# Multi-head attention with mixed heads: the softmax weights applied two steps after the scores, and q·k as three products of high and low parts

## The chip, the cores and the metric

The kernel runs on one NeuronCore of a Trainium2 chip. The metric is the time of one execution on the device, in microseconds (us); lower is better. Engines are written as the profile writes them: PE is TensorE's matmuls, PEld its weight loads, DVE is VectorE, ACT is ScalarE, POOL is GpSimd, SP is SyncE (which here only issues DMAs). Each engine executes its own instructions in program order.

## The reference, cut to what matters

Three layers follow each other: an attention with heads mixed before and after the softmax, a dense feed-forward layer, and a mixture of 8 experts. The change touches the attention alone.

```python
batch, n_heads, seq, head_dim = 4, 12, 448, 64
scores = scale * np.matmul(q, k.transpose(0, 1, 3, 2))
scores = np.einsum('bhij,hg->bgij', scores, w_pre)
scores = scores - np.max(scores, axis=-1, keepdims=True)
attn = np.exp(scores)
attn = attn / (np.sum(attn, axis=-1, keepdims=True) + 1e-09)
attn = np.einsum('bhij,hg->bgij', attn, w_post)
return np.matmul(attn, v).astype(np.float32)
```

Behind it the 1792 tokens of 768 numbers go through the dense layer (`x @ w_in`, 768 to 2048, an activation, `@ w_out`), and each token through one expert of 8 (768 to 1024 to 768).

## The kernel before

The queries of a batch are cut into tiles of 120 (three) and 88 (one), 16 tiles t in all. For each tile and each pair of heads p (six), `qk` makes two matmuls, one for each head of the pair, on rows 0 to 63 and 64 to 127 of PE's array. Both operands are float32, and each such matmul leaves two records in the trace. `qk_ev` scales the two results on ACT and DVE into `so`, and a DMA writes them to `S` in DRAM. The mixing of heads wants (query, head) on the partitions, so `relay` reads them back as `G`, three steps ahead of use (LEAD).

The rest goes by steps s of 20 queries (two units a of 10), 92 steps, 23 in a batch; four of them have 8 queries and one unit. A step's work:

- `premix`: PE, four matmuls with `wp`, mixed scores in PSUM (`psm`)
- `maxi`: DVE, the row maximum (`st`); `exp`: ACT, the exponential `E` and its sums
- `weights`: DVE, 1/sum (two short instructions), then POOL, `M` = `wq` times that, one for each unit
- `post`: PE, 32 small matmuls of `E` with `M` into `psa` (one buffer of two banks)
- `post_ev`: unit 0 by ACT, unit 1 by DVE, copies of `psa` into `AT`
- `av`, `av_ev`: PE, `AT` times the values of the tile before; a DVE copy `X` and a DMA to `x_dram`

The order is written out by hand in the loop at the end of `attention`. In round s it issues premix, maxi and exp of s, then post and post_ev of s-1, then av and qk of other tiles (lists in `at`: `qk` of tile t runs four steps and more before tile t-1 ends, `av` of a tile in the steps of the next one), then weights of s. `dma_k`, `dma_q` and `dma_v` load keys, queries and values some steps ahead. From round 89 on, `beside()` puts in the first work of the dense layer: the loads and decoding of its weights on DVE (`decode`), their splits into two float32r parts on ACT and POOL, and its first matmuls (L268, float32r, 128x128 by 128x448).

[...]

Of the kernel before, what the change touches and what calls it, by code (L numbers as in the profile page):

```python
# [6 lines left out]
F32 = mybir.dt.float32  # L7
F32R = mybir.dt.float32r
# [3 lines left out]
ALU = mybir.AluOpType  # L12
# [23 lines left out]
LEAD, AHEAD = 3, 4  # L36

def attention(tc, qT, kT, vT, w_pre, w_post, x_out, beside=None):


    nc=tc.nc
    tiles=[(b,i0,min(TI,S-i0)) for b in range(B) for i0 in range(0,S,TI)]
    steps=[]; first={}
# [4 lines left out]
    units=lambda s: range((steps[s][2]+9)//10)  # L48
# [6 lines left out]
    wf=pool(front,name="af",bufs=1,side="right"); pq=pool(front,name="pq",bufs=2,space=PS,side="right")  # L55
# [4 lines left out]
    def load_mix():  # L60
# [3 lines left out]
        for c in range(2):  # L64
# [2 lines left out]
            sel(out=x,in_=x,pattern=[[12,5],[0,12]],compare_op=ALU.is_ge,fill=0.0,base=11,channel_multiplier=-1)  # L67
            sel(out=y,in_=y,pattern=[[0,12],[-12,5]],compare_op=ALU.is_ge,fill=0.0,base=0,channel_multiplier=1)
            sel(out=y,in_=y,pattern=[[0,12],[12,5]],compare_op=ALU.is_ge,fill=0.0,base=11,channel_multiplier=-1)
    K={}; V={}; Q={}; St={}; G={}; PM={}; E={}; ST={}; M2={}; PA={}; AT={}; PV={}; QP={}; ready=set(); moved=set()  # L70
    def dma_k(b,p,n=2):
        t=wf.tile([128,2,S],F32,tag="K",bufs=6,name="K") if p%2==0 else K[b,p-1][1]
        for i in range(n): K[b,p+i]=(t[:,(p+i)%2],t)
        nc.sync.dma_start(out=t[:,p%2:p%2+n],in_=kT[b,2*p:2*p+2*n].rearrange("(p h) d s -> (h d) p s",h=2))
    def dma_v(b,h):
        t=w.tile([128,3,4,D],F32,tag="V",bufs=8,name="V")
        for i in range(3): V[b,h+i]=t[:,i]
        nc.sync.dma_start(out=t,in_=vT[b,:,h:h+3])
    def dma_q(t,z=None):
        b,i0,n=tiles[t]  # L80
        if t not in Q: Q[t]=wf.tile([128,6*TI],F32,tag="Q",bufs=2,name="Q")
        lo,hi=(0,6*n) if z is None else z
        nc.sync.dma_start(out=Q[t][:,lo:hi],in_=qT[b,:,6*i0+lo:6*i0+hi])
    def qk(t,p):
        b,i0,n=tiles[t]
        for z in range(2):
            r=slice(64*z,64*z+64)
            QP[t,p,z]=pq.tile([TI,S],F32,tag="q",name="psq")
            nc.tensor.matmul(QP[t,p,z][:n],Q[t][r,p*n:p*n+n],K[b,p][0][r],start=True,stop=True)  # L89
    def qk_ev(t,p):  # L90
# [29 lines left out]
    def weights(s):  # L120
        u=len(units(s)); st=ST[s]
        nc.vector.tensor_scalar_add(st[:,2,0:u],st[:,1,0:u],1e-9)
        nc.vector.reciprocal(st[:,3,0:u],st[:,2,0:u])  # L123
        for a in units(s):
            M2[s,a]=w.tile([124,60],F32,tag="M2",bufs=4,name="M2")
            nc.gpsimd.tensor_scalar_mul(M2[s,a],wq,st[:,3,a:a+1])  # L126
    def post(s,a):
        e,m=E.pop((s,a)),M2.pop((s,a))
        if a==0: PA[s]=pa.tile([128,2,512],F32,tag="a",name="psa")
        for cc in range(4):  # L130
            for cp in range(2):
# [4 lines left out]
    def post_ev(s,a):
        t,k,_=steps[s]
        if t not in AT: AT[t]=w.tile([128,4,12,TI],F32,tag="AT",bufs=2,name="AT")
        i=k+10*a
        o=AT[t][:,:,:,i:i+10].rearrange("p c g (r q) -> p r (c g) q",r=2)  # L140
        x=PA[s][:,:,240*a:240*a+240].rearrange("p r (m q) -> p r m q",q=5)
        if a==0: nc.scalar.copy(o,x)  # L142
        else: nc.vector.tensor_copy(o,x)  # L143
        ready.add((s,a))
    def av(t,p):
        b,i0,n=tiles[t]; l=first[t+1]-1
        if any((l,a) not in ready for a in units(l)): raise RuntimeError('values before weights')
        if p%3==0: PV[t,p//3]=pv.tile([128,3,TI],F32,tag="v",name="psv")
        ps=PV[t,p//3]
        for j in range(4):  # L150
            for z in range(2): nc.tensor.matmul(ps[64*z:64*z+64,p%3,:n],V[b,2*p+z][:,j,:],AT[t][:,j,2*p+z,:n],start=j==0,stop=j==3)  # L151
    def av_ev(t,p):
        if p%3<2: return
        b,i0,n=tiles[t]; x=w.tile([128,3,TI],F32,tag="X",bufs=3,name="X")
        nc.vector.tensor_copy(x[:,:,:n],PV.pop((t,p//3))[:,:,:n])  # L155
        nc.sync.dma_start(out=x_out[b,:,p-2:p+1,i0:i0+n],in_=x[:,:,:n])
    from collections import defaultdict
    at={k:defaultdict(list) for k in 'qakvd'}
    for t in range(NT):
        b=tiles[t][0]; n=first[t+1]-first[t]  # L160
        if t>1:
            for p in range(6): at['q'][first[t-1]-AHEAD+p*(first[t]-first[t-1])//6].append((t,p))
            at['d'][max(0,first[t-1]-AHEAD-4)].append((t,))
        m=first[t+2]-first[t+1] if t+1<NT else 3
        for p in range(6): at['a'][first[t+1]+1+p*m//6].append((t,p))
        if t%4==0 and b>0:
            for p in (0,2,4): at['k'][first[t-1]-AHEAD-9+p].append((b,p))
        if t%4==0:
            for h in (0,3,6,9): at['v'][first[t]+h//3].append((b,h))

    dma_q(0,(0,2*TI)); dma_k(0,0,1); dma_k(0,1,1); dma_q(0,(2*TI,6*TI)); dma_k(0,2); dma_k(0,4)
    dma_q(1)
    load_mix()
    for t in range(2):
        for p in range(6): qk(t,p); qk_ev(t,p)
        if t==0:
            for s in range(LEAD): relay(s)
    for s in range(0,NS+5):
        on=s<NS
        if s+LEAD<NS: relay(s+LEAD)  # L180
        for x in at['d'][s]: dma_q(*x)
        for x in at['k'][s]: dma_k(*x)
        for x in at['v'][s]: dma_v(*x)
        if on:
            premix(s)
            for a in units(s): maxi(s,a); exp(s,a)
        if 0<=s-1<NS:
# [669 lines left out]
```

## Time and profile before

| | us |
|---|---|
| median of 3 runs | 1334.84 (1334.59 to 1337.12) |
| the profiled execution, its time | 1341.98 |
| its span | 1340.3 |
| PE busy | 1217.9 (91%) |
| PEld busy | 992.6 (74%) |
| DVE busy | 787.0 (59%) |
| ACT busy | 606.5 (45%) |
| POOL busy | 312.7 (23%) |

Busy shares are means over three layers. Attention fills about the first 440 us, the beginning of the dense layer (its weights are decoded on DVE) the next 160 or so, and the dense and expert layers the rest. The profiled execution lies 7.1 us above the median of the runs.

### The profile page before, as it was taken

The numbers are of one execution on the slowest core, as the hardware profiler recorded it, in microseconds if no ns is written. First come the engines' busy times: TensorE is split into PE (matmuls) and PEld (weight loads), VectorE is DVE, ScalarE is ACT, GpSimd is POOL, SyncE is SP. The second block draws the span as 40 slices with busy tenths as digits, with TensorE's granted clock in tenths as the row PEclk, the third lists the DMA queues.
The fourth block names the chain that finished last, engine by engine and source line by source line (L and its number), as shares of the span: only waits on it lengthen the run. The fifth ranks groups of instructions, "written<-read, shape, count | busy, mean of one in ns | idle before, by whom it ended". The sixth has DMA issues, their size and how long they took to land. (4 is left out here: it accounts for less than half of the span.)

```text
span 1340.3 us, 31619 instructions
## 1 busy us (share of the span) xinstructions
PE 1217.9 (91%) x13086; PEld 992.6 (74%) x13087; DVE 787.0 (59%) x1340; ACT 606.5 (45%) x1203; POOL 312.7 (23%) x385
## 2 busy tenths in 40 slices
PE   7798998898888788779999999999996979999996
PEld 2355555555555577668899899989996979999996
DVE  1565665565655799997543544454437645566663
ACT  2455555555554444434434433443334534445552
POOL 0111111111111555553121112112113202321110
PEclk9899999999999798989999999999997989999998
DMA  7887987987966355420100010000555756656500
GB/s 222 254 242 208 296 239 212 269 254 202 281 186 203 128 203 194 152 96 26 42 22 21 1 52 11 21 1 11 183 198 172 207 160 190 190 198 228 187 20 21
DMA packets 97825, 201.09 MB, mean 150 GB/s; under 512 B 29711, under 2 KB 67733, under 8 KB 97292
## 3 DMA queue, kind: packets, MB, share of 16 engines
q1 hardware_dynamic: 91596, 186.84, 45.4%
q0 software_dynamic: 6080, 12.18, 2.9%
q8 instruction: 104, 1.70, 0.5%
q14 instruction: 45, 0.37, 0.1%
HBM read 143.60 MB, written 56.43 MB: 149 GB/s over the span
## 5 line engine op out<-in xcount | busy, mean ns | idle before, releaser
L268 PE MATMUL psh<-x,ws 128*128 128x448 f32 x1152 | 264.1, 382 | 25.2 <-POOL ws L260 14.9
L268 PEld LDWEIGHTS psh<-x,ws 128*128 128x128 f32 x1152 | 224.5, 197 | 56.0 <-POOL ws L260 20.3
L285 PE MATMUL pso<-g,ws 128*128 128x448 f32 x1152 | 252.7, 369 | 0.0
L285 PEld LDWEIGHTS pso<-g,ws 128*128 128x128 f32 x1152 | 213.8, 188 | 20.1
L135 PEld LDWEIGHTS psa<-M,E 60*64 60x64 f32 x5760 | 98.2, 138 | 115.2 <-POOL M L126 103.7
L119 ACT ACTIVATE E<-psm,st 124x448 f32<-124x448 f32 x180 | 112.5, 629 | 127.3 <-DVE st L116 127.2
L126 POOL TENSOR_SCALAR M<-wq,st 124x60 f32<-124x60 f32 x180 | 78.7, 451 | 354.8 <-DVE st L123 270.1
L260 DVE TENSOR_TENSOR ws<-res,ws 128x768 fp32r<-128x768 f32 x81 | 91.4, 1128 | 105.8 <-ACT ws L259 102.8
L135 PE MATMUL psa<-M,E 60*64 60x60 f32 x5760 | 108.9, 224 | 48.7 <-POOL M L126 43.1
L278 POOL TENSOR_TENSOR g<-th,g 128x448 fp32r<-128x448 f32 x64 | 78.4, 1225 | 308.2 <-ACT g L277 308.1
L661 PE MATMUL psh<-xt,ws 128*128 128x256 f32 (+2 forms) x1152 | 147.7, 289 | 0.1
L661 PEld LDWEIGHTS psh<-xt,ws 128*128 128x128 f32 x1152 | 145.3, 190 | 0.3 <-DVE xt L653 0.3
L628 DVE TENSOR_TENSOR ws<-res,ws 128x768 fp32r<-128x768 f32 x128 | 121.9, 959 | 39.7 <-ACT ws L627 39.5
L143 DVE COPY AT<-psa 128x480 f32<-128x480 f32 x88 | 60.2, 685 | 133.1 <-ACT AT L142 133.1
L89 PE MATMUL psq<-K,Q 64*120 64x448 f32 (+1 forms) x384 | 114.8, 648 | 11.9 <-ACT so L94 7.0
L116 DVE TENSOR_REDUCE st<-psm 124x1 f32<-124x448 f32 x180 | 103.7, 617 | 14.6 <-PE psm L112 13.8
L680 PE MATMUL psy<-ws,hh 128*128 128x384 f32 x576 | 110.4, 345 | 0.0
L627 ACT CAST ws<-res 128x768 fp32r<-128x768 f32 x128 | 105.5, 832 | 7.9 <-PE psy L697 4.9
L259 ACT CAST ws<-res 128x768 fp32r<-128x768 f32 x108 | 89.9, 832 | 35.5 <-DVE res L254 35.5
L151 PE MATMUL psv<-AT,V 128*64 128x120 f32 (+1 forms) x1536 | 98.8, 273 | 6.9 <-DVE X L155 3.5
L680 PEld LDWEIGHTS psy<-ws,hh 128*128 128x128 f32 x576 | 100.9, 190 | 0.0
L112 PE MATMUL psm<-G,wp 60*64 60x448 f32 x720 | 94.5, 578 | 0.5 <-ACT E L119 0.5
(178 smaller groups left out, 1289.5 us busy)
## 6 DMA issues: line engine op xcount, KB each, us to landing
res<-in_wm SPq DMA_DIRECT2D x56, 768.0 KB
G<-S SPq DMA_DIRECT2D x176, 210.0 KB
S<-so SPq DMA_DIRECT2D x72, 420.0 KB
wd<-in_w_in SPq DMA_DIRECT2D x10, 768.0 KB
wd<-in_w_out SPq DMA_DIRECT2D x10, 768.0 KB
S<-so SPq DMA_DIRECT2D x24, 308.0 KB
V<-in_vT SPq DMA_DIRECT2D x16, 384.0 KB
K<-in_kT SPq DMA_DIRECT2D x11, 448.0 KB
```

Source lines behind the costliest of these rows:

```text
L89: nc.tensor.matmul(QP[t,p,z][:n],Q[t][r,p*n:p*n+n],K[b,p][0][r],start=True,stop=True)
L112: nc.tensor.matmul(PM[s,a][64*c:64*c+64],wp[r],G[s][r,c,:],start=True,stop=True)
L116: nc.vector.reduce_max(ST[s][:,0,a:a+1],PM[s,a][:124],axis=AX.X,negate=True)
L119: nc.scalar.activation(E[s,a],PM.pop((s,a))[:124],AF.Exp,bias=ST[s][:,0,a:a+1],scale=1.0,accum_out=ST[s][:,1,a:a+1])
L135: nc.tensor.matmul(PA[s][64*cp:64*cp+64,c,240*a+60*cc:240*a+60*cc+60],e[r,j:j+64],m[r],start=True,stop=True)
L151: for z in range(2): nc.tensor.matmul(ps[64*z:64*z+64,p%3,:n],V[b,2*p+z][:,j,:],AT[t][:,j,2*p+z,:n],start=j==0,stop=j==3)
L268: nc.tensor.matmul(ps[:,:TB],t[:,wz,c],x[:,xz,:],start=k==0,stop=k==17); k+=1
L285: nc.tensor.matmul(OB[b][o][:,:TB],t[:,wz,c],g[:,xz,:],start=f==0 and k==0,stop=f==NF-1 and k==2)
L627: nc.scalar.copy(t[:,0,:],r[:,c])
L628: nc.vector.tensor_tensor(out=t[:,1,:],in0=r[:,c],in1=t[:,0,:].bitcast(F32),op=ALU.subtract)
L661: nc.tensor.matmul(ps,w[:,a,k*128:(k+1)*128],x[:,b,:],start=k==0 and (a,b)==(0,0),stop=k==5 and a==1)
L680: nc.tensor.matmul(PY[e][2*c+z],h[:,a,c*CP:c*CP+CP],w[:,b,z*384:z*384+384],start=f==0 and k==0,stop=f==7 and k==2)
```

## The change

- Round s now issues post and post_ev of step s-2, then weights of s-1, then av, qk and the evictions of qk. Before it was post and post_ev of s-1, av, qk, weights of s. The loop has one round more, and `av` comes one step later.
- `post_ev` is cut by c (the two banks of `psa`) instead of by unit: c=0 by ACT, c=1 by DVE, and the copies into one `AT` tile are declared independent of each other.
- For tiles 2 to 15, `qk` is six matmuls instead of two: for both heads high q by high k, then high q by low k, then low q by high k, in float32r. Tiles 0 and 1 keep the two float32 matmuls (`raw`).
- `split` makes the parts: for k of a pair of pairs (128x896) a copy on ACT and a subtraction on POOL, 12 times; for q of a tile (128x720 or 528) a copy on DVE and a subtraction on POOL, 14 times. The raw loads go to `kr` and `qr`, two rounds earlier than before; three of the k splits stand ahead of the loop.

```diff
+    def split(k,d,x,shape,bufs,n=None):
+        r=R.pop(k)
+        h,l=(wf.tile(shape,F32R,tag=x+i,bufs=bufs,name=x+i) for i in 'hl')
...
+        if x=='K': nc.scalar.copy(h,r)
+        else: nc.vector.tensor_copy(h,r)
+        nc.gpsimd.tensor_tensor(out=l,in0=r,in1=h.bitcast(F32),op=ALU.subtract)
...
-    def qk(t,p):
-        b,i0,n=tiles[t]
-        for z in range(2):
-            r=slice(64*z,64*z+64)
-            QP[t,p,z]=pq.tile([TI,S],F32,tag="q",name="psq")
-            nc.tensor.matmul(QP[t,p,z][:n],Q[t][r,p*n:p*n+n],K[b,p][0][r],start=True,stop=True)
+    def qk(t,p,raw=False):
+        b,i0,n=tiles[t]; i=slice(p*n,p*n+n)
+        for z in range(2): QP[t,p,z]=pq.tile([TI,S],F32,tag="q",name="psq")
+        if raw: pairs=((R['q',t],R['k',b,p//2]),)
+        else: (qh,ql),(kh,kl)=Q[t,],K[b,p//2]; pairs=((qh,kh),(qh,kl),(ql,kh))
+        for x,(q,k) in enumerate(pairs):
+            for z in range(2):
+                r=slice(64*z,64*z+64)
+                nc.tensor.matmul(QP[t,p,z][:n],q[r,i],k[r,p%2],start=x==0,stop=x==len(pairs)-1)
...
-        o=AT[t][:,:,:,i:i+10].rearrange("p c g (r q) -> p r (c g) q",r=2)
-        x=PA[s][:,:,240*a:240*a+240].rearrange("p r (m q) -> p r m q",q=5)
-        if a==0: nc.scalar.copy(o,x)
-        else: nc.vector.tensor_copy(o,x)
+        o=AT[t][:,:,:,k:k+10*u].rearrange("p x g (a c q) -> p a c (x g) q",c=2,q=5)[:,:,c]
+        x=PA[s][:,c,0:240*u].rearrange("p (a m q) -> p a m q",a=u,q=5)
+        e=nc.scalar.copy if c==0 else nc.vector.tensor_copy
+        i=e(o[:,0],x[:,0]) if u==1 else e(o,x)
+        for j in WA[t]: tc.declare_no_dep(i.ins,j,reason="distinct queries")
...
-            at['d'][max(0,first[t-1]-AHEAD-4)].append((t,))
+            at['d'][max(0,first[t-1]-AHEAD-6)].append((t,)); at['D'][max(0,first[t-1]-AHEAD-2)].append((t,))
...
-        for p in range(6): at['a'][first[t+1]+1+p*m//6].append((t,p))
+        for p in range(6): at['a'][first[t+1]+2+p*m//6].append((t,p))
...
-    for s in range(0,NS+5):
+    for p in (0,2,4): split_k(0,p)
+    for s in range(0,NS+6):
...
-        if 0<=s-1<NS:
-            for a in units(s-1): post(s-1,a)
-            for a in units(s-1): post_ev(s-1,a)
+        if 0<=s-2<NS:
+            for a in units(s-2): post(s-2,a)
+            for c in range(2): post_ev(s-2,c)
+        if 0<=s-1<NS: weights(s-1)
         for x in at['a'][s]: av(*x); av_ev(*x)
         for x in at['q'][s]: qk(*x)
-        if on: weights(s)
         for x in at['q'][s]: qk_ev(*x)
+        for x in at['K'][s]: split_k(*x)
+        for x in at['D'][s]: split_q(*x)
```

How the rows move is seen best where the loop begins. On PE, at the first rounds, before (psq is the result of qk, psm of premix, psa of post, and M with its number the weights of one unit of a step):

```order
L89 MATMUL psq<-K,Q 120x448 x24
L112 MATMUL psm<-G,wp 64x448 x8
L135 MATMUL psa<-M_236,E 64x60 x16
L135 MATMUL psa<-M_238,E 64x60 x16
L112 MATMUL psm<-G,wp 64x448 x4
L135 MATMUL psa<-M_296,E 64x60 x16
L135 MATMUL psa<-M_298,E 64x60 x16
L89 MATMUL psq<-K,Q 120x448 x2
```

The same place on PE in the changed kernel (Kh, Kl, Qh, Ql are the high and low parts):

```order
L102 MATMUL psq<-kr,qr 120x448 x24
L125 MATMUL psm<-G,wp 64x448 x12
L148 MATMUL psa<-M_270,E 64x60 x16
L148 MATMUL psa<-M_272,E 64x60 x16
L102 MATMUL psq<-Kh,Qh 120x448 x2
L102 MATMUL psq<-Kl,Qh 120x448 x2
L102 MATMUL psq<-Kh,Ql 120x448 x2
L125 MATMUL psm<-G,wp 64x448 x4
L148 MATMUL psa<-M_332,E 64x60 x16
```

Three premixes (12 matmuls) now run before the first post, where there were two, and a call of qk is three rows of two.

On DVE, at the same first rounds, before (st is maximum and sum, AT the copy of post, so the eviction of qk):

```order
L95 TENSOR_SCALAR so<-psq 120x448 x12
L116 TENSOR_REDUCE st<-psm 124x1 x2
L122 TENSOR_SCALAR st<-st 124x2
L123 RECIPROCAL st<-st 124x2
L116 TENSOR_REDUCE st<-psm 124x1 x2
L143 COPY AT<-psa 128x2x48x5
L122 TENSOR_SCALAR st<-st 124x2
```

and in the changed kernel:

```order
L108 TENSOR_SCALAR so<-psq 120x448 x12
L129 TENSOR_REDUCE st<-psm 124x1 x2
L80 CAST Qh<-qr 128x720
L129 TENSOR_REDUCE st<-psm 124x1 x2
L135 TENSOR_SCALAR st<-st 124x2
L136 RECIPROCAL st<-st 124x2
L129 TENSOR_REDUCE st<-psm 124x1 x2
L156 COPY AT<-psa 128x2x48x5
```

The reciprocal of a step now stands behind the maxima of the next step, and a copy of q stands between the maxima of rounds 0 and 1.

On PE, at the end of attention (psh is the dense layer's first matmul, psv is av), before:

```order
L135 MATMUL psa<-M_6913,E 64x60 x16
L151 MATMUL psv<-AT,V 64x120 x8
L135 MATMUL psa<-M_6982,E 64x60 x16
L151 MATMUL psv<-AT,V 64x120 x8
L268 MATMUL psh<-x,ws 128x448 x18
L151 MATMUL psv<-AT,V 64x88 x16
```

and in the changed kernel:

```order
L148 MATMUL psa<-M_7369,E 64x60 x16
L166 MATMUL psv<-AT,V 64x120 x8
L286 MATMUL psh<-x,ws 128x448 x18
L148 MATMUL psa<-M_7427,E 64x60 x16
L166 MATMUL psv<-AT,V 64x120 x8
L286 MATMUL psh<-x,ws 128x448 x18
```

The last post moved behind the dense layer's first 18 matmuls.

## Rows read from the trace of the kernel before

**Rows 1.** Two stretches: us, busy of PE, PEld, DVE, ACT, POOL, clock, DMA share, GB/s

```profile
42.00:428.00 386.00, 339.93 (x7828) 200.74 (x7823) 230.27 (x541) 206.01 (x514) 71.19 (x171) 0.98 0.83 236
460.00:600.00 140.00, 111.59 (x516) 94.20 (x516) 138.75 (x125) 57.58 (x81) 72.33 (x61) 0.91 0.46 165
```

**Rows 2.** Who waited for whom, us in total, times, longest: 42 to 428 us

```profile
DVE AT L143 <- ACT AT L142: 127.0, 84, 3.3
...
PE psa L135 <- POOL M L126: 35.2, 49, 1.5
...
PEld psm L112 <- DMA G<-S: 16.6, 25, 0.7
...
PEld psa L135 <- issue: 11.0, 26, 1.9
```

**Rows 3.** Timeline, 262 to 268 us: start, duration, instruction, idle before and its releaser

```profile
262.49 0.98 PE L112 MATMUL psm<-G,wp 60*64 60x448 f32 x8
...
263.57 1.16 DVE L116 TENSOR_REDUCE st<-psm 124x1 f32<-124x448 f32 x2
...
265.53 0.64 ACT L142 COPY AT<-psa 128x480 f32<-128x480 f32 x1
...
266.20 0.69 DVE L143 COPY AT<-psa 128x480 f32<-128x480 f32 x1 [1.47 <-ACT AT L142]
...
267.32 0.83 POOL L126 TENSOR_SCALAR M<-wq,st 124x60 f32<-124x60 f32 x2 [3.28 <-DVE st L123]
...
267.81 0.33 PEld L135 LDWEIGHTS psa<-M,E 60*64 60x64 f32 x16 [1.12 <-POOL M L126]
```

**Rows 4.** Timeline of PE, 300 to 312 us: one step without a wait

```profile
307.64 0.98 PE L112 MATMUL psm<-G,wp 60*64 60x448 f32 x8
308.44 1.11 PE L135 MATMUL psa<-M,E 60*64 60x60 f32 x64
309.48 1.04 PE L151 MATMUL psv<-AT,V 128*64 128x120 f32 x16
310.45 1.02 PE L89 MATMUL psq<-K,Q 64*120 64x448 f32 x4
311.40 0.98 PE L112 MATMUL psm<-G,wp 60*64 60x448 f32 x8
```

**Rows 5.** Groups of instructions by form, 42 to 428 us: busy us, mean ns, idle before

```profile
L112 PE MATMUL psm<-G,wp 60*64 60x448 f32 x678 | 87.0, 571 | 0.0
...
L89 PE MATMUL psq<-K,Q 64*120 64x448 f32 x240 | 64.4, 604 | 1.9 <-ACT so L94 1.9
...
L112 PE MATMUL psm<-G,wp 36*64 36x448 f32 x6 | 2.9, 562 | 0.0
```

**Rows 6.** The page's costliest groups: dense layer's float32r matmuls and splits

```profile
L285 PE MATMUL pso<-g,ws 128*128 128x448 f32 x1152 | 252.7, 369 | 0.0
L285 PEld LDWEIGHTS pso<-g,ws 128*128 128x128 f32 x1152 | 213.8, 188 | 20.1
...
L259 ACT CAST ws<-res 128x768 fp32r<-128x768 f32 x108 | 89.9, 832 | 35.5 <-DVE res L254 35.5
```

**Rows 7.** Timeline, 0 to 48 us: the first loads and the first rounds

```profile
1.30 0.89 SPq L74 DMA_DIRECT2D K<-in_kT  x2
...
4.04 1.85 PE L89 MATMUL psq<-K,Q 64*120 64x448 f32 x4 [4.04 <-DMA K<-in_kT]
...
39.70 0.42 SPq L83 DMA_DIRECT2D Q<-in_qT  x1
...
40.77 1.14 DVE L116 TENSOR_REDUCE st<-psm 124x1 f32<-124x448 f32 x2
```

**Rows 8.** Timeline, 415 to 475 us: the end of attention

```profile
445.42 1.82 POOL L260 TENSOR_TENSOR ws<-re,ws 128x768 fp32r<-128x768 f32 x1
...
447.20 1.84 POOL L228 TENSOR_TENSOR x<-xs,x 128x448 fp32r<-128x448 f32 x1
...
453.51 4.70 PE L268 MATMUL psh<-x,ws 128*128 128x448 f32 x18
```

More of the change, by code (lines that the diff above doesn't have):

```diff
@@ L69, in load_mix, with split_k, split_q @@
             sel(out=y,in_=y,pattern=[[0,12],[12,5]],compare_op=ALU.is_ge,fill=0.0,base=11,channel_multiplier=-1)
-    K={}; V={}; Q={}; St={}; G={}; PM={}; E={}; ST={}; M2={}; PA={}; AT={}; PV={}; QP={}; ready=set(); moved=set()
+    R={}; K={}; V={}; Q={}; St={}; G={}; PM={}; E={}; ST={}; M2={}; PA={}; AT={}; PV={}; QP={}; WA={}; ready=set(); moved=set()
     def dma_k(b,p,n=2):
-        t=wf.tile([128,2,S],F32,tag="K",bufs=6,name="K") if p%2==0 else K[b,p-1][1]
-        for i in range(n): K[b,p+i]=(t[:,(p+i)%2],t)
-        nc.sync.dma_start(out=t[:,p%2:p%2+n],in_=kT[b,2*p:2*p+2*n].rearrange("(p h) d s -> (h d) p s",h=2))
+        if p%2==0: R['k',b,p//2]=wf.tile([128,2,S],F32,tag="kr",bufs=3,name="kr")
+        nc.sync.dma_start(out=R['k',b,p//2][:,p%2:p%2+n],in_=kT[b,2*p:2*p+2*n].rearrange("(p h) d s -> (h d) p s",h=2))
+    def split(k,d,x,shape,bufs,n=None):
+        r=R.pop(k)
+        h,l=(wf.tile(shape,F32R,tag=x+i,bufs=bufs,name=x+i) for i in 'hl')
+        if n is not None: r,h,l=r[:,:n],h[:,:n],l[:,:n]
+        if x=='K': nc.scalar.copy(h,r)
+        else: nc.vector.tensor_copy(h,r)
+        nc.gpsimd.tensor_tensor(out=l,in0=r,in1=h.bitcast(F32),op=ALU.subtract)
+        d[k[1:]]=(h,l)
+    def split_k(b,p): split(('k',b,p//2),K,'K',[128,2,S],6)
+    def split_q(t): split(('q',t),Q,'Q',[128,6*TI],2,6*tiles[t][2])
     def dma_v(b,h):
@@ L80, in dma_q @@
         b,i0,n=tiles[t]
-        if t not in Q: Q[t]=wf.tile([128,6*TI],F32,tag="Q",bufs=2,name="Q")
+        if ('q',t) not in R: R['q',t]=wf.tile([128,6*TI],F32,tag="qr",bufs=2,name="qr")
         lo,hi=(0,6*n) if z is None else z
-        nc.sync.dma_start(out=Q[t][:,lo:hi],in_=qT[b,:,6*i0+lo:6*i0+hi])
-    def qk(t,p):
-        b,i0,n=tiles[t]
-        for z in range(2):
-            r=slice(64*z,64*z+64)
-            QP[t,p,z]=pq.tile([TI,S],F32,tag="q",name="psq")
-            nc.tensor.matmul(QP[t,p,z][:n],Q[t][r,p*n:p*n+n],K[b,p][0][r],start=True,stop=True)
+        nc.sync.dma_start(out=R['q',t][:,lo:hi],in_=qT[b,:,6*i0+lo:6*i0+hi])
+    def qk(t,p,raw=False):
[7 more added lines that the diff above has]
+                nc.tensor.matmul(QP[t,p,z][:n],q[r,i],k[r,p%2],start=x==0,stop=x==len(pairs)-1)
     def qk_ev(t,p):
@@ L135, in post, with post_ev @@
                     nc.tensor.matmul(PA[s][64*cp:64*cp+64,c,240*a+60*cc:240*a+60*cc+60],e[r,j:j+64],m[r],start=True,stop=True)
[L136 to L139, printed above, removed]
-        o=AT[t][:,:,:,i:i+10].rearrange("p c g (r q) -> p r (c g) q",r=2)
-        x=PA[s][:,:,240*a:240*a+240].rearrange("p r (m q) -> p r m q",q=5)
-        if a==0: nc.scalar.copy(o,x)
-        else: nc.vector.tensor_copy(o,x)
-        ready.add((s,a))
+    def post_ev(s,c):
+        t,k,n=steps[s]; u=len(units(s))
+        if t not in AT: AT[t]=w.tile([128,4,12,TI],F32,tag="AT",bufs=2,name="AT"); WA[t]=[]
+        o=AT[t][:,:,:,k:k+10*u].rearrange("p x g (a c q) -> p a c (x g) q",c=2,q=5)[:,:,c]
[3 more added lines that the diff above has]
+        for j in WA[t]: tc.declare_no_dep(i.ins,j,reason="distinct queries")
+        WA[t].append(i.ins)
+        ready.add((s,c))
     def av(t,p):
         b,i0,n=tiles[t]; l=first[t+1]-1
-        if any((l,a) not in ready for a in units(l)): raise RuntimeError('values before weights')
+        if any((l,c) not in ready for c in range(2)): raise RuntimeError('values before weights')
         if p%3==0: PV[t,p//3]=pv.tile([128,3,TI],F32,tag="v",name="psv")
@@ L157, in attention @@
     from collections import defaultdict
-    at={k:defaultdict(list) for k in 'qakvd'}
+    at={k:defaultdict(list) for k in 'qakvdKD'}
     for t in range(NT):
@@ L162, in attention @@
             for p in range(6): at['q'][first[t-1]-AHEAD+p*(first[t]-first[t-1])//6].append((t,p))
-            at['d'][max(0,first[t-1]-AHEAD-4)].append((t,))
+            at['d'][max(0,first[t-1]-AHEAD-6)].append((t,)); at['D'][max(0,first[t-1]-AHEAD-2)].append((t,))
         m=first[t+2]-first[t+1] if t+1<NT else 3
-        for p in range(6): at['a'][first[t+1]+1+p*m//6].append((t,p))
+        for p in range(6): at['a'][first[t+1]+2+p*m//6].append((t,p))
         if t%4==0 and b>0:
-            for p in (0,2,4): at['k'][first[t-1]-AHEAD-9+p].append((b,p))
+            for p in (0,2,4): at['k'][first[t-1]-AHEAD-11+p].append((b,p)); at['K'][first[t-1]-AHEAD-7+p].append((b,p))
         if t%4==0:
@@ L174, in attention @@
     for t in range(2):
-        for p in range(6): qk(t,p); qk_ev(t,p)
+        for p in range(6): qk(t,p,True); qk_ev(t,p)
         if t==0:
             for s in range(LEAD): relay(s)
-    for s in range(0,NS+5):
+    for p in (0,2,4): split_k(0,p)
+    for s in range(0,NS+6):
         on=s<NS
```

## The prediction

> **What bounds the kernel now.** I read the stretches of the trace first, then the waits, then the timeline of single steps. From 42 to 428 us the kernel does little but attention steps: PE is busy 340 of 386 us, DVE 230, ACT 206, POOL 71, and the DMA engines 0.83 of the time [rows 1]. No engine is full, and the sum at which I look is the step. premix leaves 8 records a step, 4 in the one short step of each 23, so 7.83 on the mean; 678 and 6 records [rows 5] are 87.4 steps, and 386 / 87.4 = **4.42 us a step**.
>
> PE itself needs less. In a step where nothing was late, premix to post is 0.80 us, post 1.04, av 0.97, qk 0.95, together 3.76 [rows 4]. av and qk run 84 times in 88 steps (14 tiles by 6), so PE's own work is about 0.80 + 1.04 + 0.95 x 1.92 = 3.66 us a step. The other 0.76 us are waits.
>
> The waits name the chain. DVE sits 127.0 us behind ACT at L143, 84 times: each time its half of the copy into AT waits for ACT's half [rows 2]. One step shows what follows [rows 3]: premix of a step at 262.49, its maxima until 264.73, then exp, then ACT's copy at 265.53 (it stands behind two exps), DVE's copy at 266.20, and only behind that the step's sum and reciprocal, POOL's M at 267.32, and its post at 267.81. So post of a step comes 5.32 us behind its premix; the next premix but one stands behind post, av and qk (3.76 - 0.80 = 2.96 us), which closes a loop of 8.3 us over two steps, 4.14 us a step. Late G, two qk in one round and the X copies add the rest.
>
> Behind it, from 460 to 600 us, DVE is busy 138.75 of 140 us [rows 1]: decoding of weights. It is the bound there, so attention that ends earlier lets the rest start earlier, one for one.
>
> **The change, part by part.**
>
> *Post two steps late.* The step's own chain through max, exp, reciprocal and M no longer stands before its post. What remains between premix of s and post of s-1: the maxima of s end 2.24 us behind premix, then DVE's copy of post(s-2) (0.69) and the reciprocal of s-1; from the start of the copy to M took 1.12 us, from M to post 0.49 [rows 3]. So post(s-1) can start 3.85 us behind premix(s), and premix(s+2) 2.96 us later: 6.8 us for two steps, 3.4 a step. This is below PE's own work, so PE becomes the bound.
>
> *The copies cut by bank, independent.* The 127.0 us of DVE waits go; ACT and DVE copy the same number of elements as before. DVE's copy then waits for PE's post alone, which is over before the maxima are.
>
> *q·k in three products.* No row shows float32r matmuls on half the rows. In the float32 form the two heads run side by side: a float32 record of 448 columns lasts 604 ns [rows 5], a float32r record of the dense layer 369 [rows 6], and the difference is about one more pass at the dense layer's pace of 252.7 us / 1152 = 0.22 us; so a record holds two passes, and the four of a call, one behind the other, would take 8 x 0.22 = 1.76 us. They take 0.95 [rows 4]. If float32r does the same, three pairs at 0.20 to 0.22 and some margin at the change from one shape to the next (the float32 form has 0.95 - 4 x 0.22 = 0.07; I allow up to 0.19) make 0.67 to 0.85; I take 0.80, a gain of 0.15 us a call. Bounds: 0.66 (no margin) and 6 x 0.22 + 0.19 = 1.51 (one behind the other). PE's own work becomes 0.80 + 1.04 + 0.95 x (0.97 + 0.80) = **3.52 us**.
>
> [...]
>
> *What still waits.* G that lands late cost 16.6 us, and pauses in PE's own issue 11.0 [rows 2]; they have nothing to do with M, and I keep them: 27.6 / 87.4 = 0.32 us a step.
>
> *The splits.* A k split is a copy of 128x896 on ACT (832 ns for 768 columns [rows 6], so 0.97) and a subtraction on POOL (1.82 for 768 [rows 8], so 2.12); POOL can hold M back by at most that, nine times in the loop. A q split puts a copy of 720 columns on DVE ahead of the next maxima; not shown, bounded by zero and by the 0.69 us of the 480-column copy [rows 3], scaled 1.03. Together at most 9 x 2.12 + 14 x 1.03 = 34 us, at least nothing where the slack of a step hides them. POOL is busy a fifth of the time and M now has a step's slack, so I take 9 us, 0.1 a step. Loads of k and q are issued four rounds ahead of their split; G only three ahead of its use, so G is late first.
>
> So a step takes 3.52 + 0.32 + 0.10 = **3.94 us**, and 87.4 steps gain 0.48 each: 42 us. DMA allows it: 0.83 of 4.42 us is 3.67 us of transfers a step [rows 1], and no byte is added.
>
> *The start.* Ahead of the loop stand three k splits, 6.4 us on POOL, and in round 0 DVE copies q of tile 2, whose load is issued at 39.70 us [rows 7]. The first k load was issued at 1.30 and read at 4.04, 2.7 us later; the maxima of step 1, at 40.77 before, come some 3 us later. M of step 0 stands behind those 6.4 us and 1.7 for q, but its post is now two rounds away. I take 3 us (0 to 8).
>
> *The end.* The weights of the last two steps stand in POOL's queue behind the dense layer's splits, 1.8 us each [rows 8], and the last post behind 18 dense matmuls, 4.70 us [rows 8]; DVE stands waiting at its copies meanwhile, and DVE is what the next 140 us hang on. Against that its waits for ACT go. I take a loss of 4 us (0 to 12).
>
> **The sum**: -42 + 3 + 4 = -35 us. Against the profiled execution's 1341.98 that is 1307; the runs lie 7.1 lower, so **1300 us**.
>
> **The rivals.**
>
> *DMA becomes the bound.* From 42 to 428 us it is at 0.83 with bursts of k, q and v on top of S and G. The late G of [rows 2] grows as steps shorten, since G is issued three steps ahead whatever a step lasts. At 0.83 / 4.15 x 4.42 = 0.88 mean share a step would be 4.15 us: gain 24, less 7, 1318 us. For it: the 25 late G already. Against: they cost only 16.6 us.
>
> *All waits go.* If late G and the splits hide too, a step comes down to the 3.67 us of transfers: gain 65 us, 1270 to 1275. Against it speaks that pauses of PE's issue are no wait that the change touches.
>
> *Serial products (slower).* If the two heads' float32r matmuls don't run side by side, a call is 1.51 us, PE's work 3.52 + 0.95 x 0.71 = 4.19, a step 4.61: 17 us lost, and 7 at the ends, 1359. It decides from a call of about 1.2 us on (a step of 4.34). For it: no row shows them side by side; against: the float32 form does it.
>
> *Loads shown.* With 0.19 us for each of three pairs a call is 0.80 + 0.57 = 1.37, a step 4.48, and the time about 1347. The 0.22 us pace of loads and matmuls on the same rows [rows 6] speaks against it. [...]
>
> *Given back.* A step of 4.3 us and an end that costs 10 leave the time where it was: 1335.
>
> **How the numbers follow.** Forecast (steps of 3.85 to 4.05 us, 1291 to 1310): 0.45. DMA: 0.25. All waits go, or most: 0.15. Given back: 0.05. Serial: 0.06. Loads shown: 0.04. A measurement here can tell about 0.2% (2.7 us). Faster: 0.45 + 0.25 + 0.15 = 0.85; the same 0.05; slower 0.10. The range leaves out the slower cases and half of the upper part of "given back" and reaches down to the transfers' bound: 1272 to 1326.
>
> **What would show it.** Right: steps of 3.85 to 4.05 us; DVE's wait for ACT at the AT copy near zero; PE's wait for M below 10 us; qk calls of 0.75 to 0.85 us with six records; DMA share above 0.9. Wrong: PE waiting for G in most steps (DMA), qk calls above 1.2 us (serial, loads shown), M behind long subtractions on POOL, or DVE waits of over 10 us between the last step and the first uninterrupted decoding.

## The result, and the profile after

The median of six runs is 1322.33 us, against 1336.7 us for the kernel before beside it: a ratio of 0.9894 [0.9873, 0.9914], 14.4 us faster. Disturbed executions, here one of the changed kernel at 1650.5 us, stay in the medians of this document and are left out of its ratios; the other five lie between 1318.85 and 1326.15 us. The forecast was 35 us faster. The time lies in the range, 22 us above the number.

I follow the gain through the program at two marks: the first and the last premix, and the first decoding into `res` on DVE, where the decoding that nothing interrupts begins. The view of one line's groups gives the times of the first and last start. Before:

```profile
L112 PE MATMUL psm<-G,wp x720: 536/587/1006, 36.6 to 440.9; 60*64 60x448 f32 x180
...
L251 DVE TENSOR_SCALAR res<-wd x15: 727/1518/1953, 472.2 to 609.9; 128x768 int32<-128x768 int32 x15
```

After, the same view:

```profile
L125 PE MATMUL psm<-G,wp x720: 532/587/1006, 36.9 to 405.8; 60*64 60x448 f32 x180
...
L269 DVE TENSOR_SCALAR res<-wd x15: 553/1521/1953, 452.4 to 589.5; 128x768 int32<-128x768 int32 x15
```

The last premix comes 35.1 us earlier, the first decoding only 19.8. From there to the end of the span it takes 868.1 us before (1340.3 - 472.2) and 868.3 after (1320.7 - 452.4). So the steps gained about what was forecast, and **15 us were lost between the last step and the decoding**. Everything behind it moved along one for one.

The stretches that answer to [rows 1] (us; busy of PE, PEld, DVE, ACT, POOL; clock, DMA share, GB/s):

```profile
42.00:393.00 351.00, 319.06 (x7881) 222.82 (x7876) 244.74 (x553) 210.93 (x516) 115.62 (x194) 0.98 0.89 259
460.00:600.00 140.00, 114.30 (x483) 97.10 (x483) 138.72 (x123) 57.71 (x83) 73.91 (x60) 0.91 0.38 139
```

PE is now busy 0.91 of the attention, and the DMA engines 0.89. The waits of 42 to 393 us, which answer to [rows 2]:

```profile
PEld psa L148 <- issue: 43.9, 118, 4.3
...
PEld psa L148 <- POOL M L139: 20.8, 44, 1.3
PE psa L148 <- issue: 19.6, 14, 4.2
...
DVE Qh L80 <- DMA qr<-in_qT: 6.7, 1, 6.7
...
PEld psm L125 <- DMA G<-S: 3.6, 10, 0.7
...
PE psa L148 <- POOL M L139: 2.1, 4, 0.6
```

DVE's wait for ACT at AT (127.0 us in [rows 2]) is gone, G is late for 3.6 us instead of 16.6, and PE waits 2.1 us for M instead of 35.2. What grew are pauses of "issue", in which PE waits for nothing that the profile shows: at post 11.0 us in the queue of loads before, 43.9 now. About half of these 43.9 us are some hundred pauses of 0.22 us or so, one in most steps; on the matmuls of post 5.3 us show before and 19.6 now.

The timeline of after shows such a pause, a step without one, and the end (start, duration, instruction, idle before):

```profile
149.12 1.03 PE L148 MATMUL psa<-M,E 60*64 60x60 f32 x57
154.37 0.48 PE L148 MATMUL psa<-M,E 60*64 60x60 f32 x7 [4.22 <-issue]
154.79 1.44 PE L166 MATMUL psv<-AT,V 128*64 128x88 f32 x16
...
254.66 0.46 PE L102 MATMUL psq<-Kh,Qh 64*120 64x448 f32 x2
254.76 0.18 PEld L102 LDWEIGHTS psq<-Kl,Qh 64*120 64x120 f32 x2
254.96 0.37 PE L102 MATMUL psq<-Kl,Qh 64*120 64x448 f32 x2
255.17 0.36 PE L102 MATMUL psq<-Kh,Ql 64*120 64x448 f32 x2
255.46 0.98 PE L125 MATMUL psm<-G,wp 60*64 60x448 f32 x8
...
256.26 1.11 PE L148 MATMUL psa<-M,E 60*64 60x60 f32 x64
257.30 0.83 PE L166 MATMUL psv<-AT,V 128*64 128x88 f32 x16
258.06 0.46 PE L102 MATMUL psq<-Kh,Qh 64*120 64x448 f32 x2
258.86 0.98 PE L125 MATMUL psm<-G,wp 60*64 60x448 f32 x8
...
421.50 4.69 PE L286 MATMUL psh<-x,ws 128*128 128x448 f32 x18
426.11 0.69 PE L148 MATMUL psa<-M,E 60*64 60x60 f32 x32
426.87 0.42 DVE L156 COPY AT<-psa 128x240 f32<-128x240 f32 x1 [6.10 <-PE psa L148]
445.20 4.72 PE L286 MATMUL psh<-x,ws 128*128 128x448 f32 x18
449.85 1.43 PE L166 MATMUL psv<-AT,V 128*64 128x88 f32 x32
451.33 0.43 DVE L170 COPY X<-psv 128x264 f32<-128x264 f32 x1 [7.56 <-PE psv L166]
```

The first piece is one post, torn into 57 and 7 matmuls by 4.2 us. Behind it av takes 1.44 us, where it takes 0.83 at 257.30. The ten microseconds around it, in the columns of the stretches above:

```profile
150.00:160.00 10.00, 5.78 (x82) 3.78 (x78) 3.09 (x9) 2.53 (x6) 0.84 (x2) 0.67 0.82 251
```

The granted clock was 0.67 on the mean: 1.00 from 149.5 to 153.0 us, while PE stood idle from 150.15 on, and 0.50 from 153.5 to 160.0. The second piece is a call of qk: three pairs from 254.66 to 255.46, exactly the 0.80 us taken. The step from 255.46 to 258.86 is 3.40 us, with an av of 88 columns; in [rows 4] one with 120 columns takes 3.76. The third piece is the end. Eighteen dense matmuls stand ahead of the last post, and eighteen again ahead of the last av; DVE waits 6.10 us behind the first and 7.56 us behind the second.

### The profile page after: what moved, and what is told of

It reads as the page before. It is cut to its first block, busy times and chain, and to the rows that moved or that the text cites. A ratio compares the mean times of both kernels' runs of the same rounds, so it can differ in the third digit from the quotient of the medians.

```text
span 1320.7 us, 32107 instructions
## 1 busy us (share of the span) xinstructions
PE 1202.7 (91%) x13254; PEld 1019.6 (77%) x13255; DVE 804.5 (61%) x1358; ACT 615.9 (47%) x1215; POOL 359.7 (27%) x411
## 5 line engine op out<-in xcount | busy, mean ns | idle before, releaser
L286 PE MATMUL psh<-x,ws 128*128 128x448 f32 x1152 | 265.0, 383 | 35.0 <-ACT ws L277 19.6
L148 PEld LDWEIGHTS psa<-M,E 60*64 60x64 f32 x5760 | 107.2, 139 | 77.4 <-issue 45.8
L148 PE MATMUL psa<-M,E 60*64 60x60 f32 x5760 | 111.5, 223 | 30.5 <-issue 20.8
L108 DVE TENSOR_SCALAR so<-psq 120x448 f32<-120x448 f32 (+1 forms) x96 | 59.8, 623 | 75.5 <-PE psq L102 64.3
L125 PE MATMUL psm<-G,wp 60*64 60x448 f32 x720 | 98.7, 592 | 6.5 <-ACT E L132 5.9
L166 PEld LDWEIGHTS psv<-AT,V 128*64 128x64 f32 x1536 | 78.1, 142 | 14.8 <-issue 5.7
```

Of the source, the lines that this page charges most:

```text
L286: nc.tensor.matmul(ps[:,:TB],t[:,wz,c],x[:,xz,:],start=k==0,stop=k==17); k+=1
```

## The experiments

All were run beside the kernel before, on several chips, so compare ratios: before took 1336.0 us beside before_again and the three runs with "only", 1337.3 beside the next three and no_v_loads, 1349.2 beside slots_shift to copies_spread, and 1344.7 in one execution beside the two with half_g. "Step" is last less first premix over 91; res is the first decoding into `res`. These marks come from one profiled execution of each kernel.

| run | ratio to before | median us | last premix | step | res |
|---|---|---|---|---|---|
| before | – | 1336.7 | 440.9 | 4.44 | 472.2 |
| before_again | – | one at 1339.55 | 439.3 | 4.42 | 470.8 |
| after | 0.9894 [0.9873, 0.9914] | 1322.33 | 405.8 | 4.05 | 452.4 |
| copies_only | 0.9828 [0.9803, 0.9854] | 1312.46 | 406.3 | 4.05 | 437.3 |
| slots_only | 0.9885 [0.9864, 0.9906] | 1321.75 | 405.5 | 4.05 | 453.3 |
| parts_only | 1.0055 [1.0033, 1.0076] | 1343.68 | 442.4 | 4.45 | 475.8 |
| tail_mm | 0.9841 [0.9819, 0.9862] | 1313.91 | 404.8 | 4.04 | 443.4 |
| tail_shift | 0.9794 [0.9776, 0.9812] | 1310.53 | 404.1 | 4.04 | 440.0 |
| start | 0.9880 [0.9858, 0.9902] | 1320.99 | 399.7 | 3.98 | 444.2 |
| slots_shift | 0.9799 [0.9751, 0.9846] | 1321.93 | 408.7 | 4.08 | 443.3 |
| copies_parts | 0.9814 [0.9774, 0.9854] | 1321.92 | 408.6 | 4.09 | 439.5 |
| shift_start | 0.9786 [0.9751, 0.9821] | 1319.41 | 405.8 | 4.05 | 441.5 |
| copies_spread | 0.9780 [0.9738, 0.9823] | 1320.44 | 410.4 | 4.11 | 442.6 |
| half_g_copies | not comparable | – | 395.1 | 3.96 | – |
| half_g_parts | not comparable | – | 383.0 | 3.82 | – |
| no_v_loads | not comparable | – | 399.2 | 3.97 | – |

**The kernel before again (before_again).**

> The kernel before once more, for its profile. The trace of before that the prediction rests on came from an execution 5 to 7 us above the median of the runs. If that execution was slow by chance, this one has a span of 1333 to 1337 us and its last premix at 434 to 437 us (440.1 there). If a profiled execution of this kernel is always slower, the span is again near 1340.

Its profiled execution took 1339.55 us, 3.5 above the 1336.0 us of the others; the one shown ahead of the prediction stood 5.3 above the 1336.7. That of after stood 0.1 above its own median. So some 5 us of the 19.6 by which the spans differ aren't in the medians. Why profiled executions of before run longer stays open.

**The copies alone (copies_only)**: two slots, float32 qk, the order of before.

```diff
-            for a in units(s-1): post_ev(s-1,a)
+            for c in range(2): post_ev(s-1,c)
...
+        for j in WA[t]: tc.declare_no_dep(i.ins,j,reason="distinct queries")
```

> Only post_ev is changed: by bank instead of by unit, the copies into one AT tile independent; order and products of before. My theory: the copies were the late part of the chain. Without DVE's wait for ACT, the reciprocal stands behind the exps alone: premix to post falls from 5.3 to about 4.1 us and the loop of two steps from 8.3 to 7.1, 3.55 a step, below PE's own work of 3.66. So this edit alone gives most of the body's gain, 25 to 38 us, without the loss at the end: 1298 to 1312 us. Rival: the wait for ACT is only replaced by one for the exps of the same step, and the post has to be moved two steps: 1328 to 1337 us.

**Three slots and the copies (slots_only)**: after with the two float32 matmuls of qk, and no splits.

> Three slots and the copies by bank, but q by k stays two float32 matmuls and there are no splits. My theory: the gain in the body comes from M no longer being waited for, and the three products add little. PE's own work is then 3.66 us a step instead of 3.52, the splits' 0.1 is saved, so the step is within 0.1 us of the changed kernel's and the time 1318 to 1328 us, the loss at the end included. Rival: the body's gain comes from the shorter products; then this kernel is at 1332 to 1345 us.

**The products alone (parts_only)**: split and qk of after, order and copies of before.

> The three products and the splits, with the order and the copies of before. My theory: post still waits for M in the loop of two steps, so a call of 0.80 us instead of 0.95 frees PE only to wait longer: 1334 to 1343 us, PE's wait for M above 40 us. Rival: PE's own work is what a step costs, and 84 calls times 0.15 us come off: 1322 to 1327 us.

copies_only reaches the last premix at the same time as after (406.3 and 405.8 us), and loses nothing at the end: 31.0 us to the decoding, 31.3 before, 46.6 after. So this edit alone is enough for the gain of the body; its 1312 us are the upper end of what was expected. The cut by bank and the declared independence, its two halves, were not run apart, nor three slots with the old copies. Its waits, 42 to 393 us:

```profile
PEld psa L135 <- POOL M L126: 34.3, 77, 1.5
PEld psa L135 <- issue: 30.9, 69, 2.6
...
PE psa L135 <- issue: 17.8, 14, 2.5
...
PE psa L135 <- POOL M L126: 1.7, 3, 0.7
```

M stands in the loads' queue longer than after (34.3 against 20.8), but it reaches the matmuls for 1.7 us only: with the copies free, two slots are enough. slots_only has the step of copies_only and the loss of after (47.8 us to the decoding). parts_only keeps the chain of [rows 3], in its waits from 42 to 428 us:

```profile
DVE AT L156 <- ACT AT L155: 128.5, 83, 3.4
...
PE psa L148 <- POOL M L139: 43.1, 62, 3.8
```

A shorter qk there only makes PE wait longer for M (35.2 in [rows 2]); the kernel is 0.5% slower than before, just above the range expected. What of that the splits cost wasn't taken apart.

**The end: dense matmuls two to three places later (tail_mm).** In the list of early work of the dense layer, its first three entries of matmuls move behind other entries (decoding and splits among them) that stood after them.

```diff
-(9,'l',(0,)),
...
-(10,'l',(1,)),
...
-(14,'l',(2,)),
...
+(11,'l',(0,)), (12,'l',(1,)), (17,'l',(2,))
```

> The changed kernel with the dense layer's first three groups of 18 matmuls issued one round later, behind the last posts and av of attention; nothing else is moved. My theory: the 15 us lost between the last premix and the uninterrupted decoding are DVE's copies waiting in order for the last post and the last av, which stand on PE behind 18 dense matmuls each (waits of 6.1 and 7.6 us). They should fall to 1 to 3 us together: 8 to 12 us faster than the changed kernel, 1310 to 1315 us. Rival: the loss comes from M standing in POOL's queue behind the dense layer's splits; then 1319 to 1323.

**The end: all early work one round later (tail_shift)**, as far from the last post as before the change: it begins in round 89, counted from 0, instead of 88.

```diff
-        if s+LEAD>=NS-1 and beside is not None:
+        if s+LEAD>=NS and beside is not None:
```

> The changed kernel with all the dense layer's early work (loads, decoding, splits, matmuls) one round later, so that it stands to the last posts as before. If the order at the end is the loss, whichever part of it, the loss falls from 15 us to about 4, but the decoding starts some 3 us later: 1311 to 1317 us. If only the matmuls matter it is no better than moving these alone. Rival: the end's loss is not order but a transfer that lands late (decoding's first weights); then it is as the changed kernel or worse, 1321 to 1327.

Both show the loss to be made of order in the main. From the last premix to the decoding it takes 38.6 us with the matmuls alone moved and 35.9 with all moved, against 46.6. The time falls by 1.0% with tail_shift, whose interval [0.9776, 0.9812] lies wholly below that of after. Its end on PE:

```profile
418.06 1.13 PE L148 MATMUL psa<-M,E 60*64 60x60 f32 x32 [3.33 <-POOL M L139]
419.12 1.87 PE L166 MATMUL psv<-AT,V 128*64 128x120 f32 x16
420.92 4.48 PE L286 MATMUL psh<-x,ws 128*128 128x448 f32 x18
```

The last post stands ahead of the dense matmuls again. The stretches from the last premix to the decoding (columns as above), in before, after and tail_shift:

```profile
440.90:472.20 31.30, 22.87 (x267) 18.79 (x264) 24.80 (x31) 13.62 (x22) 18.59 (x13) 0.72 0.41 135
...
405.80:452.40 46.60, 31.24 (x368) 26.12 (x365) 29.93 (x40) 16.99 (x29) 19.69 (x15) 0.74 0.36 123
...
404.10:440.00 35.90, 25.61 (x349) 21.50 (x346) 28.55 (x36) 15.44 (x25) 19.60 (x15) 0.76 0.46 158
```

DVE is busy 24.80, 29.93 and 28.55 us in them and idle 6.5, 16.7 and 7.4. Of the 4.6 us that remain in tail_shift against before, some 3.8 are more work of DVE, as one more post and its copies stand behind the last premix, and 0.9 are idle time.

**The start (start)**: q of tile 2 is split in round 1 instead of round 0.

```diff
-at['D'][max(0,first[t-1]-AHEAD-2)].append((t,))
+at['D'][max(1,first[t-1]-AHEAD-2)].append((t,))
```

> The changed kernel with the split of tile 2's q in round 1 instead of round 0. My theory: the maxima of step 1 come 6 us late because DVE waits for that load (6.7 us in the trace), which costs 4.4 us at the first qk; a round later most of the wait is hidden behind step 1's maxima: 2 to 5 us faster than the changed kernel, 1317 to 1320. Rival: the first rounds wait for G and the loads anyway, 1321 to 1323.

DVE's wait of 6.7 us for this load no longer stands at line 80, and the fourth premix starts at 49.1 us, where it starts at 53.2 in after. But at step 20 the two are level (119.6 and 119.5 us), so the 6.1 us by which the last premix comes earlier in this profile arise later, where its granted clock was 1.00 (after 0.97). The timed runs (1314.9 to 1325.37 us) don't tell the kernel from after either, and shift_start, with the same edit, has its last premix where after has it. A gain is not shown.

**What the floor of the steps is.** copies_only, slots_only and after come to 4.05 us a step, though PE's own work differs by the 0.15 us of a call. Two runs took away or moved transfers of v; three put the repairs together; two left out score reads.

no_v_loads uses the values of batch 0 in all batches:

```diff
+        if b>0:
+            for i in range(3): V[b,h+i]=V[0,h+i]
+            return
```

> The changed kernel without the loads of the values of batches 1 to 3 (they use those of batch 0), 12 of 16 transfers of 384 KB left out. My theory: what is left of the waits in the body are pauses of PE's own issue (45.5 us at post in the load queue, 20.8 at PE, against 11.0 and 5.3 before) that come where the DMA engines are full, mostly while values are loaded (near 150, 245 and 340 us). Without the loads these pauses fall to 10 to 25 us at the load queue, and the time by 8 to 16 us, to 1306 to 1314. Rival: the pauses belong to PE's longer instruction stream and not to the transfers: they stay above 35 us and the time within 4 us of the changed kernel.

Other values send other tokens to the experts, so only the attention is read: the last premix comes 6.6 us earlier than in after, a step of 3.97. The pauses at the loads of post are 37.7 us from 42 to 393 us (43.9 in after), on the rival's side of the forecast. start, with all loads of v, has a step of 3.98, so this run doesn't show that they cost anything.

copies_spread is copies_only with the values loaded every second round:

```diff
-at['v'][first[t]+h//3]
+at['v'][first[t]+2*(h//3)]
```

> copies_only with the four loads of a batch's values issued every second round instead of every round; same bytes. My theory: the long pauses of PE's issue in the body, and the half clock that follows them, come where values, keys, G and S fill the DMA engines at once. Spread, the pauses at post (17.4 us at PE in copies_only) fall below 10 and the time by 3 to 8 us: 1304 to 1309. Rival: the pauses come whenever PE's stream is fetched, burst or not: within 3 us of copies_only.

The pauses stay (16.0 us on PE's post from 60 to 370 us, 15.0 in copies_only), and the step is no shorter (4.11). The ratio is lower than that of copies_only, but the intervals overlap. Nothing speaks for the bursts of v.

slots_shift is slots_only with the end of tail_shift; copies_parts is copies_only with the products and the start of start; shift_start is after with both repairs.

> Three slots and the copies by bank, float32 products, and the dense layer's early work one round later: against copies_only (1312 us) it shows what the three slots give in the body when the end costs nothing. My theory now: nothing, since with the copies freed M comes in time in two slots as well, and PE's own work is the bound in both: 1308 to 1315 us. Rival: the third slot still removes PE's wait for M (30 us at the load queue in copies_only), worth 5 to 12 us: 1300 to 1307 us.

> The copies by bank with the three products and the splits (that of tile 2's q a round later), in the two slots of before. My theory: PE's own work falls by 0.14 us a step, but two slots leave M no slack behind POOL's long subtractions, so at most half of 12 us comes: 1304 to 1312 us. Rival one: M in two slots is the bound again, 1313 to 1320. Rival two: the products' gain comes in full, 1298 to 1303.

> The changed kernel with both repairs: the dense layer's early work one round later, and the split of tile 2's q in round 1. If the two losses are separate, 12 us of the one and 2 to 5 of the other come off: 1304 to 1309 us. If the start's gain was an accident of one execution, it is at 1309 to 1312 like the shift alone.

These three and copies_spread lie between 0.978 and 0.981, with intervals of 0.004 to 0.005 either way that overlap. With or without the products, with two slots or three, these runs can't tell the kernels apart once the end costs little.

half_g_copies and half_g_parts are copies_only and shift_start, in which the odd step of a pair doesn't load its scores:

```diff
+        if s%2 and steps[s-1][2]>=steps[s][2]: G[s]=G[s-1]; return
         G[s]=w.tile([124,2,S],F32,tag="G",bufs=6,name="G")
```

> This is the kernel that changes the copies alone (two slots, one float32 call), and in it the odd step of a pair of equal size uses the score addend G of the even step before it, so about half of those transfers are left out. That changes the computation (other tokens reach other experts), so the whole time can't be compared; read is only the attention body up to the last premix (406 us with all G). Theory, the fullness of the DMA engines is the common floor of about 4.0 us a step: the last premix falls to 372 to 382 us (3.70 to 3.80 us a step, PE's own 3.66 and little else), and the pauses of PE's issue at post fall below 8 us (17.4 us with all G). Rival, the pauses belong to PE's own stream of instructions: the last premix stays at 395 or later, and the pauses at 12 us or more.

> The changed kernel with the two repairs (the rounds of the early items shifted by one, q of tile 2 split in round 1), and here too the odd step of a pair of equal size uses the even step's G, which changes the computation; read is only the attention body up to the last premix (406 us with all G). Theory, DMA fullness is the floor: the last premix falls to 358 to 372 us, 3.55 to 3.70 us a step, some 10 us before that of the kernel with the copies alone, since PE's own work is 3.52 us and not 3.66: the gain of the products then shows. Rival, PE's own stream: 395 us or later, pauses at 12 us or more, and no difference between the two kernels.

The stretch from 60 to 370 us in after:

```profile
60.00:370.00 310.00, 284.98 (x7050) 200.87 (x7044) 219.22 (x494) 189.18 (x462) 102.99 (x171) 0.97 0.90 265
```

in half_g_copies:

```profile
60.00:370.00 310.00, 297.66 (x7188) 189.68 (x7188) 222.76 (x497) 188.27 (x470) 64.45 (x155) 1.00 0.77 219
```

and in half_g_parts:

```profile
60.00:370.00 310.00, 293.31 (x7462) 206.94 (x7462) 229.25 (x518) 197.75 (x486) 107.31 (x181) 0.99 0.77 221
```

In it, the waits at PE's matmuls of post in half_g_parts, where after has 18.4 us in 12 pauses:

```profile
PE psa L149 <- issue: 4.8, 6, 1.5
```

**What the pauses are.** The view of the DMA queues of after has a queue q8 of kind "instruction" with 106 packets of 16 KB in the whole span (packets, MB, share of 16 engines):

```profile
q8 instruction: 106, 1.74, 0.5%
```

Asked for three tenths of a microsecond (each packet begins in its tenth), from 151.8, 240.1 and 334.5 us, it shows

```profile
q8 instruction: 1, 0.02, 67.9%
...
q8 instruction: 1, 0.02, 59.3%
...
q8 instruction: 1, 0.02, 70.6%
```

A share of 67.9% of 16 engines in 0.1 us is 1.09 us for the packet, so it lands at about 152.9; the other two land at 241.1 and 335.7. The pause that is torn into post at 149.12 ended at 154.37, 1.4 to 1.5 us behind the landing. The other two, in the timeline:

```profile
242.42 0.73 PE L148 MATMUL psa<-M,E 60*64 60x60 f32 x34 [1.61 <-issue]
...
337.05 0.68 PE L148 MATMUL psa<-M,E 60*64 60x60 f32 x28 [2.08 <-issue]
```

They end 1.3 and 1.4 us behind theirs. So it is with each of the 13 pauses of over 0.5 us at post's loads in after (55 to 400 us): all end 1.3 to 1.65 us behind the landing of such a packet, though one comes only every 5.4 us on the median. It holds beyond these: all 247 pauses of "issue" on PE's matmuls from 60 to 370 us, in all sixteen traces and whatever the matmul, end 1.2 to 1.75 us behind the landing of such a packet, where a moment picked blindly does so less than one time in ten. From this timing alone I take it that PE stands without instructions until its next packet of code has come; the view gives the kind of the queue, not the engine that it serves. Most of the packets cost nothing that shows: of the 55 that land from 60 to 370 us in after, 15 end a pause, 20.1 us together.

With half of the score reads the pauses at post fall to 4.8 us (6.4 in half_g_copies), the step to 3.96 us with float32 and 3.82 us with the products. Each is one execution, but the ten kernels with freed copies and all reads take 362.6 to 373.6 us from first to last premix, and these two 360.0 and 347.5. The same stretch in four kernels, of the same work for PE in each pair: first copies_only and half_g_copies, then shift_start and half_g_parts:

```profile
37.30:406.30 369.00, 341.21 (x8127) 215.05 (x8128) 253.35 (x566) 213.76 (x532) 75.06 (x177) 0.99 0.88 259
...
35.10:395.10 360.00, 340.68 (x8129) 214.24 (x8128) 254.37 (x569) 214.43 (x535) 74.77 (x178) 0.99 0.75 216
...
37.00:405.80 368.80, 337.73 (x8215) 235.32 (x8216) 256.64 (x576) 222.16 (x544) 122.36 (x202) 0.97 0.87 256
...
35.50:383.00 347.50, 328.22 (x8217) 228.42 (x8216) 255.52 (x576) 221.43 (x544) 122.38 (x202) 1.00 0.76 221
```

With all reads copies_only and shift_start are level (369.0 and 368.8 us); with half of them the two are 12.5 us apart, what 84 calls at 0.15 us less would give (12.6). The pair differs in the slots too, but PE is idle 19.3 us in both, so the whole 12.5 us stand in PE's busy time (340.68 and 328.22). With all reads PE's busy time differs by 3.5 us only. The pauses on all of PE's matmuls fall in both kernels, from 21.6 to 13.2 us with float32 and from 24.4 to 13.2 with the products; with the products 9.5 us of busy time go besides. Part of these goes with the clock, 0.97 in shift_start and 1.00 in half_g_parts; start, at 1.00 with all reads, is busy 333.4 us. The rest is not explained.

The steps that were expected (3.70 to 3.80, and 3.55 to 3.70) didn't come: my count of PE's work took qk and av as a mean over the loop. In half_g_copies 80 calls (320 records by 4) fall on 78.2 steps (606 + 6 premix records by 7.83) in the window from 60 to 370 us, 0.80 + 1.04 + 1.92 x 1.02 = 3.80 us, and PE was busy 297.66 / 78.2 = 3.81 us a step. There PE's own work is nearly all of the step. So with half of the score reads PE pauses less for what I take to be late code (13.2 us in both kernels), and the shorter qk shows. A packet of code takes 1.0 to 1.1 us on the median with all reads and with half of them, so the late ones begin late: that behind the pause of 4.2 us began when PE had stood for some 1.7 us. Why they do (a full engine ahead of it, or SP's own issues, which the edit takes away too) is not shown.

## Why the prediction was wrong, step by step

- **The step that failed: "The end".** I took a loss of 4 us (0 to 12) and named the cause, M behind splits and the last post behind 18 dense matmuls. It measured 15.3 us (46.6 - 31.3). I counted one wait of DVE behind 4.70 us of dense matmuls [rows 8]; there were two, of 6.10 and 7.56 us, at the last copy into AT and at the last X. In all 10.2 of the 15.3 us are more idle time of DVE (16.7 - 6.5) and 5.1 more work that it had left behind the last premix (29.93 - 24.80), which I had not counted. tail_mm gives 8 us of it back by moving the matmuls alone, tail_shift 10.7.
- **The body, -42 + 3 us.** It measured 35.1 us, start included: right in amount. A step took 4.05 us where I had 3.94 and the start. In the profile of start it was 3.98, with pauses as long on all of PE's matmuls (19.4 us from 60 to 370 us, 20.1 in after) but a granted clock of 1.00 there, 0.97 in after.
- **Where the body's gain comes from.** I gave it to three edits: the M chain cut by the third slot, the copies, and qk. copies_only shows that the copies alone are enough for it. My loop of 8.3 us over two steps held DVE's wait for ACT's copy as one link (1.47 us in [rows 3]); without that link two slots suffice, and the third bought nothing that these runs can tell and brought the loss at the end (slots_only 47.8 us, copies_only 31.0).
- **q·k in three products.** The call was 0.80 us as taken, and "Serial products" and "Loads shown", which adds a load of [rows 6] (188 ns) to each of the three pairs, are refuted. The second and third pair start 0.30 and 0.21 us behind the one ahead, though each loads weights for rows that are at work: the loads of the second start at 254.76 and take 0.18 us, and the matmuls of the first run from 254.66 to 255.12. But the 0.14 us a step that I booked for it (some 12 us) don't appear while all reads are there.
- **What still waits, 0.32 us, and the splits, 0.10.** The sum held (PE was idle 31.9 us from 42 to 393 us, 0.37 us a step), the content didn't. I kept G's lateness (16.6 us) and the pauses of 11.0; G's fell to 3.6 and the pauses rose to 43.9 in the loads' queue. I had taken them for a fixed cost of PE's issue, and read them in the queue of loads, of which less than half shows on the matmuls (5.3 of the 11.0, 19.6 of the 43.9). About half of the 43.9 us are short ones of 0.22 us; the long ones, 19.6 us on PE's matmuls of post, are late code by their timing, and fall with half of the score reads. The rival "DMA becomes the bound" (1318 us) was right about the traffic and looked in the wrong place: not G comes late but, by the timing of the pauses, PE's instructions.
- **The start, 3 us.** DVE waited 6.7 us for q of tile 2, and the maxima of step 1 came at 46.98 us, 6.2 later than in [rows 7]; by the fourth premix it was 4.3 us (53.2 and 48.9).
- **The base.** I laid the gain of one profiled execution on the median. Of the 20.6 us missed (35 less 14.4), 11.3 are the end, 3.9 the body with its start, 0.2 lies behind the decoding mark, and 5.2 are that the profiled execution of before stood 5.3 us above its median and that of after 0.1.

copies_only, tail_mm, tail_shift, slots_shift, copies_parts, shift_start and copies_spread, at 0.978 to 0.984 of before, lie below both kernels with their whole intervals.

## What to carry to other kernels

When the profile shows a queue standing in a wait between two engines' halves of one copy, make the halves independent first and measure, before deepening the pipeline: that alone was enough for the whole gain here. A deeper pipeline ends later by its own depth, and every list of work that is tied to a round number must move with it. A shorter operation on the busiest engine showed here only where there were fewer transfers: 12.5 us from the first to the last premix with half of the score reads, 0.2 us with all.

## What was not expected of the hardware

- By its timing PE's code comes as DMA traffic: in after a packet of 16 KB every 5.4 us on the median, and PE pauses for up to 4.2 us between two matmuls of one group, with no wait that the profile shows, until 1.2 to 1.75 us behind the landing of such a packet. From 60 to 370 us such pauses on all of PE's matmuls sum to 8 to 9 us in before and before_again, at a DMA share of 0.85, and 7 in parts_only at 0.87, where PE waits for M as well; to 16 in no_v_loads (0.87), 19 to 24 in the ten kernels with freed copies and all reads (0.88 to 0.90), and 10 and 13 with half of the score reads (0.77). The share alone doesn't order them.
- A pause can be paid twice: at the one of 4.2 us in after the granted clock fell from 1.00 to 0.50 and stayed there from 153.5 to 160.0 us, and av took 1.44 instead of 0.83 us. In shift_start each of the five stretches of 10 us at a clock of 0.85 or less (from 60, 120, 150, 250 and 340 us) holds such a pause of 2.3 to 3.4 us or follows one; start has pauses of up to 2.3 us at a clock of 1.00, so not each is paid twice.
- Two float32r matmuls on the two halves of the rows ran side by side in after: two records of 460 ns within 0.46 us at 254.66, and six in a call of 0.80 us. So did the float32 ones in before: four records of 584 ns on the mean within 1.02 us at 310.45, in a call of 0.95.
